# Re-slotting the weight conversion and softmax steps of a fused attention and MoE kernel, with 20 low-bit steps on ScalarE

## The chip, the cores and the metric

The kernel runs on one core of one Trainium2 chip. The metric is the device time of one execution, in microseconds (us); lower is better. The kernel before takes 794.07 us, the median of three runs (793.29 to 794.18).

## What is computed

The reference is a pooled attention followed by a gated two-layer product. Cut to what matters:

```
k_p = k.reshape(B, H, 72, 8, 64).mean(axis=3)        # B, H, S, D = 8, 8, 576, 64
v_p = v.reshape(B, H, 72, 8, 64).mean(axis=3)
attn = softmax(q @ k_p.T / sqrt(D)) @ v_p            # (B, H, S, D)
x = attn.transpose(0, 2, 1, 3).reshape(4608, 512)
a, b = x @ w1, x @ w2                                # w1, w2: 512 x 1024
out = (a * b) @ w3 @ w_out                           # w3: 1024 x 1024, w_out: 1024 x 512
```

The four weights arrive as 64-bit floats (20 MB in all); q, k and v are 32-bit floats.

## The kernel before, in words

**Chunks.** The 4608 tokens are worked in 12 chunks of 384. For chunk `m` TensorE (PE in the profile) does eight column blocks `j`: `a_mm` (12 matmuls, line 584), `b_mm` (12, line 584) and, one block later, `out_mm` (9, line 619). Every f32 operand is split into a high part, rounded to the matmul's type, and a low remainder, and a product is three passes: high by high, high by low, low by high. `w3 @ w_out` does not depend on the tokens, so it is folded first into one 1024 x 512 matrix `W`: 16 steps `s` of `w_mm` (line 645, 12 matmuls each), steps 0 to 7 for its first half, 8 to 15 for its second. Attention of chunk `n` (`s_mm` line 392, softmax, the transposes `pt_mm` line 454 and `ptr_mm` line 464, `av_mm` lines 558 to 561) is worked among the column blocks of chunk `n - 1`; that of chunk 0 stands among the steps `w_mm` 8 to 15.

**Weights.** Forty tiles of 512 KB (16 of `w3`, 8 of `w_out`, called wo, 16 of w1 and w2 together, called w12) are loaded as pairs of 32-bit words and turned into f32. For each tile `high` (ScalarE, ACT, line 135) takes sign, exponent and upper mantissa from the upper word, `low` (VectorE, DVE, line 140) takes the top three bits of the lower word by a shift of 29, and `conv_b` (VectorE, line 148) shifts the first by three and joins them. Then a `w3` tile is transposed on TensorE (`w_turn`, line 206); the high part is a ScalarE cast (lines 185, 192 and 152) and the low part a subtraction, on VectorE for `w3` and wo (lines 194, 177, 153) and, for 13 of the 16 w12 tiles, on GpSimd (POOL, line 153; `LO_DVE` lists the three others). In the first half of the product, `w_block` (lines 164 to 194) issues these steps of three neighbouring tiles as one fixed group.

**Softmax.** `soft1` takes the scores of four heads from PSUM: a minimum on VectorE (line 408), then either subtraction (line 410, VectorE), one Exp (413, ScalarE) and one sum (414, VectorE), or, for the tiles in `SOFT_ACT`, four Exp with bias and accumulated sum on ScalarE alone (line 418). `soft2` normalises (427 to 430, VectorE), `soft3` copies and splits the eight rest keys (442 ScalarE, 444 VectorE).

**k and v.** Eight neighbouring keys are summed, by three GpSimd additions (`pool_tree`, lines 348 to 350) or, for the k tiles in `K_DVE`, by one VectorE reduction (line 308). v's remainder (the eight pooled keys past the first 64) comes in eight loads of 16 KB per batch (`load_vr`, line 345) and becomes the tile `VR` (line 379, GpSimd).

**What sets the order.** Everything is put into a list `plan` with `at(kind, k, fn, ...)`, where `k` is a time slot; the list is sorted by slot and then by kind (loads, post-processing, main matmuls, attention matmuls) and issued in that order. Every engine runs its own instructions in that order, so an instruction that waits holds up all those behind it on its engine. All loads are issued from SyncE (SP), in order, and each waits for the load eight places before it to have landed. Three PSUM buffers (`patt`, name `att`) serve all transposes, scores and attention outputs, so a matmul into one waits until the reader of the old content is done.

Of the kernel before, what the change touches and what calls it, by code (L numbers as in the profile page):

```python
# [18 lines left out]
def kernel(  # L19
# [117 lines left out]
    def low(c, r):  # L137

        w = c.rearrange("p (c t) -> p c t", t=2)
        nc.vector.tensor_scalar(out=r, in0=w[:, :, 0], scalar1=29, scalar2=None, op0=ALU.logical_shift_right)  # L140
# [23 lines left out]
    def w_block(v):  # L164


        new, mid, old = v < NJ, 0 <= v - 1 < NJ, 0 <= v - 2 < NJ
        if new:
            w_tiles(v)
            r3, z3 = stage["w3", v]  # L170
            ro, zo = stage["wo", v]
            high(raw["w3", v], z3)
            low(raw.pop(("w3", v)), r3)
            high(raw["wo", v], zo)
        if old:
            s = v - 2
            nc.vector.tensor_tensor(out=wo[s][1], in0=f(stage["wo", s][0]), in1=f(wo[s][0]), op=ALU.subtract)  # L177
        if new:
            if v > 0:
                low(raw["wo", v], ro)  # L180
            conv_b(r3, z3)
        if mid:
            ps = w_turn(v - 1)
            w3t[v - 1] = hl_cell(4 + (v - 1) % 4)
            nc.scalar.copy(out=w3t[v - 1][0], in_=ps)
        if new:
            if v == 0:
                low(raw["wo", v], ro)
            conv_b(ro, zo)
        if mid:  # L190
            wo[v - 1] = hl_cell(8 + v - 1)
            nc.scalar.copy(out=wo[v - 1][0], in_=f(stage["wo", v - 1][0]))
        if mid:
            nc.vector.tensor_tensor(out=w3t[v - 1][1], in0=ps, in1=f(w3t[v - 1][0]), op=ALU.subtract)
# [7 lines left out]
    def w_turn(s):  # L202
        r = f(stage.pop(("w3", s))[0])
        ps = patt.tile([P, 512], F32, tag="att", name="att")
        for it in range(4):
            nc.tensor.transpose(out=ps[:, it * P:(it + 1) * P], in_=r[:, it * P:(it + 1) * P], identity=ident)
        return ps

    def w_conv(s):
        w_tiles(s)  # L210
        conv_a(raw.pop(("w3", s)), *stage["w3", s])

    def w_conv2(s):
        conv_b(*stage["w3", s])

    def w_split(s):
        ps = w_turn(s)
        w3t[s] = hl_cell(4 + s % 4)
        split(ps, *w3t[s])

    def w12_conv(j, w):
# [116 lines left out]
    def load_vr(b):  # L338
        t = stage["vr", b] = st_tile([P, 2, POOL, D])
        for g in range(2):  # L340
            for r in range(4):
# [3 lines left out]
                nc.sync.dma_start(out=t[KR * r:KR * r + KR, g].rearrange("k e d -> k (e d)"), in_=src)

    def pool_tree(t, dst):
        nc.gpsimd.tensor_tensor(out=t[:, :, 0:4], in0=t[:, :, 0:4], in1=t[:, :, 4:8], op=ALU.add)  # L348
        nc.gpsimd.tensor_tensor(out=t[:, :, 0:2], in0=t[:, :, 0:2], in1=t[:, :, 2:4], op=ALU.add)  # L349
# [469 lines left out]
```

## Time and profile before

| | before |
|---|---|
| median of three runs | 794.07 us |
| the profiled execution's own time | 796.23 us |
| its span, first to last instruction | 794.4 us |
| matmuls on TensorE | 4122 |
| VectorE busy | 457.4 us (58%) |
| ScalarE busy | 272.1 us (34%) |
| GpSimd busy | 210.0 us (26%) |
| loads and stores | 80.12 MB |

Times in the views are microseconds from the start of the span, unless marked ns. A group's row has its line, engine, operation, what it writes and reads, its count, its busy time and the mean duration of one, and behind the second bar the idle time of the engine ahead of it and what ended that. PEclk is the TensorE clock that was granted, as a share of full speed. In the timeline a bracket at the end of a row is the idle time ahead of it and what ended it. `raw` is a loaded weight tile, `Wc`, `wt` and `wb` are work tiles for `w3`, wo and w12, and `hl` is a finished weight in its high and low halves.

### The profile page before, as it was taken

What the parts mean: (1) busy time and instruction counts of PE and PEld (TensorE: products, weight loads), DVE (VectorE), ACT (ScalarE), POOL (GpSimd) and SP (SyncE); (2) the same over time, 40 slices, a digit from 0 to 9 for tenths busy, and PEclk for the clock granted to TensorE, in tenths of its full rate; (3) what the DMA queues carried; (4) which work ended last, traced back from release to release, by engine and by line L of the source; (5) the groups of instructions that cost most, each with busy time, mean ns of one, the idle gap of its engine ahead of it and who ended that gap; (6) DMA issues with size and microseconds to landing.
All of it is one profiled execution on the core that took longest, in us unless ns stands there. A gap on an engine that the chain in (4) does not pass through costs nothing.

```text
span 794.4 us, 11422 instructions
## 1 busy us (share of the span) xinstructions
PE 762.6 (96%) x4122; PEld 705.9 (89%) x4122; DVE 457.4 (58%) x889; ACT 272.1 (34%) x625; POOL 210.0 (26%) x240
## 2 busy tenths in 40 slices
PE   7888888999999999999999999999999999999998
PEld 7667778999999898999998998999998998999997
DVE  5866999565565465574384474474565664653111
ACT  5556555432233232333233223223323223323211
POOL 1153555402506413021408303022227221000000
PEclk9998999999999999999999999999999999999999
DMA  9896981024625412326326322138235314130101
GB/s 331 230 232 166 264 173 22 1 71 118 117 71 143 90 51 76 60 71 152 83 70 155 80 92 71 23 106 167 64 97 110 106 53 89 45 94 10 40 1 40
DMA packets 128680, 80.12 MB, mean 101 GB/s; under 512 B 82544, under 2 KB 112432, under 8 KB 128624
## 3 DMA queue, kind: packets, MB, share of 16 engines
q1 hardware_dynamic: 128624, 79.40, 39.7%
q8 instruction: 32, 0.52, 0.3%
q14 instruction: 24, 0.20, 0.1%
HBM read 61.08 MB, written 18.28 MB: 100 GB/s over the span
## 4 chain that ended last, share of the span: by engine, by line
PE 66%; DVE 9%; POOL 7%; DMA 7%; issue 4%; ACT 4%; SPq 2%; POOLq 0%; ACTq 0%; DVEq 0%
PE o L619 19%; PE a L584 19%; PE b L584 19%; DMA raw<-in_moe_w_dram 4%; PE att L392 3%; POOL st L348 3%; POOL VR L379 1%; DMA st<-in_k_dram 1%; POOL st L349 1%; PE att L561 1%; PE o L645 1%; DMA raw<-in_moe_w_out_dram 1%; DVE E L430 1%; PE att L559 1%; PE att L560 1%
## 5 line engine op out<-in xcount | busy, mean ns | idle before, releaser
L584 PE MATMUL a<-xT,hl 128*128 128x384 f32 x1152 | 222.6, 342 | 0.0
L584 PE MATMUL b<-xT,hl 128*128 128x384 f32 x1152 | 220.3, 339 | 0.0
L584 PEld LDWEIGHTS a<-xT,hl 128*128 128x128 f32 x1152 | 207.0, 191 | 6.1
L584 PEld LDWEIGHTS b<-xT,hl 128*128 128x128 f32 x1152 | 200.2, 189 | 0.0
L619 PE MATMUL o<-Wc,gh 128*128 128x512 f32 x576 | 183.6, 400 | 1.8 <-ACT gh L605 1.8
L348 POOL TENSOR_TENSOR st<-st 72x512 f32<-72x512 f32 (+2 forms) x53 | 76.8, 1448 | 248.6 <-DMA st<-in_k_dram 192.4
L604 DVE TENSOR_TENSOR a<-b,a 128x384 f32<-128x384 f32 x96 | 53.2, 554 | 124.8 <-PE b L584 124.2
L619 PEld LDWEIGHTS o<-Wc,gh 128*128 128x128 f32 x576 | 105.1, 189 | 19.9 <-ACT gh L605 2.8
L619 PE MATMUL o<-Wc,gl 128*128 128x512 f32 x288 | 114.2, 397 | 0.0
L594 ACT COPY a<-a 128x384 f32<-128x384 f32 x96 | 46.0, 479 | 173.0 <-PE a L584 152.0
L605 ACT CAST gh<-a 128x384 fp32r<-128x384 f32 x96 | 49.5, 515 | 154.5 <-DVE a L604 154.4
L610 DVE TENSOR_TENSOR gl<-a,gh 128x384 fp32r<-128x384 f32 x96 | 65.7, 684 | 39.1 <-ACT gh L605 38.5
L619 PEld LDWEIGHTS o<-Wc,gl 128*128 128x128 f32 x288 | 54.1, 188 | 13.4 <-DVE gl L610 0.9
L570 DVE TENSOR_TENSOR xT<-att,xT 128x384 fp32r<-128x384 f32 x48 | 26.6, 556 | 57.5 <-ACT xT L569 57.5
L413 ACT ACTIVATE E<-E 128x288 f32<-128x288 f32 (+1 forms) x70 | 31.2, 446 | 80.3 <-DVE E L410 80.3
L392 PE MATMUL att<-kbd,qT 128*128 128x144 f32 (+1 forms) x320 | 53.7, 292 | 3.4 <-DVE mx L408 3.2
L392 PEld LDWEIGHTS att<-kbd,qT 128*128 128x128 f32 (+1 forms) x320 | 48.2, 183 | 5.8 <-ACT E L418 4.0
L414 DVE TENSOR_REDUCE sm<-E 128x4 f32<-128x288 f32 (+1 forms) x70 | 31.6, 452 | 36.7 <-ACT E L413 36.7
L408 DVE TENSOR_REDUCE mx<-att 128x4 f32<-128x288 f32 (+1 forms) x80 | 35.4, 444 | 28.5 <-PE att L392 28.5
L361 POOL TENSOR_TENSOR vbd<-vm,vbd 64x256 fp32r<-64x256 f32 x16 | 12.4, 777 | 147.3 <-ACT vbd L360 147.2
L645 PE MATMUL o<-hl 128*128 128x512 f32 x144 | 43.0, 441 | 4.6 <-DVE hl L177 4.5
L349 POOL TENSOR_TENSOR st<-st 72x256 f32<-72x256 f32 (+2 forms) x53 | 42.9, 809 | 4.2
(91 smaller groups left out, 758.3 us busy)
## 6 DMA issues: line engine op xcount, KB each, us to landing
raw<-in_moe_w_dram SPq DMA_DIRECT2D x32, 512.0 KB
st<-in_k_dram SPq DMA_DIRECT2D x32, 288.0 KB
out_dram<-ob SPq DMA_DIRECT2D x35, 256.0 KB
st<-in_v_dram SPq DMA_DIRECT2D x32, 256.0 KB
qs<-in_q_dram SPq DMA_DIRECT2D x128, 48.0 KB
D<-T SPq DMA_DIRECT2D x7, 768.0 KB
PTl<-D SPq DMA_DIRECT2D x28, 192.0 KB
raw<-in_moe_w_out_dram SPq DMA_DIRECT2D x8, 512.0 KB
```

Source lines behind the costliest of these rows:

```text
L348: nc.gpsimd.tensor_tensor(out=t[:, :, 0:4], in0=t[:, :, 0:4], in1=t[:, :, 4:8], op=ALU.add)
L349: nc.gpsimd.tensor_tensor(out=t[:, :, 0:2], in0=t[:, :, 0:2], in1=t[:, :, 2:4], op=ALU.add)
L392: nc.tensor.matmul(out=ps[:nt, 2 * KP * j:2 * KP * (j + 1)], lhsT=qT[n][:, pr, off:off + nt], rhs=kbd[b % 2][:, pr], start=True, stop=True,)
L408: nc.vector.tensor_reduce(out=mx[:nt, hs], in_=sv, axis=AX.X, op=ALU.min)
L414: nc.vector.reduce_sum(out=sm[:nt, hs], in_=E[:nt, hs], axis=AX.X)
L584: nc.tensor.matmul(out=o, lhsT=w12[j, w][sw][:, kt * P:(kt + 1) * P], rhs=x[sx][:, kt], start=(i == 0), stop=(i == 3 * NK - 1))
L594: nc.scalar.copy(out=a, in_=gt[m, j][:, :CH])
L604: nc.vector.tensor_tensor(out=g, in0=ps[:, :CH], in1=g, op=ALU.mult)
L605: nc.scalar.copy(out=gh, in_=g)
L610: nc.vector.tensor_tensor(out=gl, in0=g, in1=f(gh), op=ALU.subtract)
L619: nc.tensor.matmul(out=oacc[m][t], lhsT=(gh, gl)[sg][:, c], rhs=W[j][sw], start=(j == 0 and i == 0), stop=(j == NJ - 1 and i == 2))
L645: nc.tensor.matmul(out=wacc[h][it], lhsT=w3t[s][sa][:, it * P:(it + 1) * P], rhs=wo[j][sb], start=(j == 0 and i == 0), stop=(j == NJ - 1 a ...
```

## The change

Four things are changed; the matmuls and what they multiply stay as they are.

1. What was one step becomes several, each with its own slot: `w_block`, `w_conv` and `w_split` become `r3_high`, `r3_low`, `r3_conv`, `w_turn`, `w3_hi`, `w3_lo` for `w3` and `ro_high` to `ro_lo` for wo; w12 gets `t_high` to `t_lo`; softmax `soft1`, `soft_e`, `soft_s`, `soft3`, `soft4`; x, g and v's remainder likewise. A table `SHIFT` adds a number to the slot of single steps, and `at` looks it up. Its entries belong to chunks 0 and 1, to the weights, and to the k and v of batches 0 and 1; the later chunks keep their order.
2. `low` has a second form on ScalarE: it reads one byte of each 8-byte element and scales it. 20 of the 40 tiles take it (8 of `w3`, 4 of wo, 8 of w12).
3. Other steps change engine: four wo remainders go from VectorE to GpSimd, w12 remainders on GpSimd become 9 instead of 13, k tile (1, 1) goes to GpSimd, k tile (0, 2) to VectorE additions, softmax tiles (0, 2) and (1, 2) from four Exp on ScalarE to VectorE and one Exp, tile (1, 0) the other way.
4. v's remainder comes in 4 loads of 32 KB per batch instead of 8 of 16 KB, and the mask `msk` is made by way of a ScalarE step.

```diff
-    SOFT_ACT = [(0, 0), (0, 1), (0, 2), (1, 1), (1, 2)]
-    LO_DVE = [(0, 1), (4, 1), (6, 0)]
-    K_DVE = [(0, 1), (1, 1), (1, 3)]
+    SOFT_ACT = [(0, 0), (0, 1), (1, 0), (1, 1)]
+    LO12_POOL = [(0, 0), (2, 0), (2, 1), (3, 0), (4, 0), (5, 0), (5, 1), (6, 0), (7, 0)]
+    LOW_ACT = [('w12', 0, 0), ('w12', 0, 1), ('w12', 1, 0), ('w12', 1, 1), ('w12', 2, 0), ('w12', 3, 1), ('w12', 5,
+        1), ('w12', 6, 1), ('w3', 0), ('w3', 1), ('w3', 13), ('w3', 5), ('w3', 6), ('w3', 7), ('w3', 8), ('w3', 9),
+        ('wo', 0), ('wo', 1), ('wo', 6), ('wo', 7)]
+    LOO_POOL = [1, 2, 4, 7]
+    K_RED = [(0, 1), (1, 3)]
+    K_TREE = [(0, 2)]
...
+    one = stp.tile([P, P], I32, tag="st", name="one")
+    nc.scalar.activation(out=one, in_=ident, func=AF.Copy, scale=0.75, bias=0.0)
...
-    def low(c, r):
-
+    def low(c, r, act=False):
+
+        if act:
+            b = c.bitcast(U8).rearrange("p (c t) -> p c t", t=8)
+            nc.scalar.activation(out=r, in_=b[:, :, 3], func=AF.Copy, scale=2.0 ** -5, bias=-31.0 / 64)
+            return
...
-    def conv_a(c, r, z):
-        high(c, z)
-        low(c, r)
-
...
+    def r3_low(s):
+        low(raw.pop(("w3", s)), stage["w3", s][0], ("w3", s) in LOW_ACT)
+
+    def r3_conv(s):
+        conv_b(*stage["w3", s])
...
+    def ro_lo(s):
+        eng = nc.gpsimd if s in LOO_POOL else nc.vector
+        eng.tensor_tensor(out=wo[s][1], in0=f(stage["wo", s][0]), in1=f(wo[s][0]), op=ALU.subtract)
...
+    def w3_hi(s):
+        w3t[s] = hl_cell(4 + s % 4)
+        nc.scalar.copy(out=w3t[s][0], in_=tp[s])
...
     def load_vr(b):
         t = stage["vr", b] = st_tile([P, 2, POOL, D])
-        for g in range(2):
-            for r in range(4):
...
+        for r in range(4):
+            par = r % 2
+            src = v[b, r::4, RK0[par] * POOL:(RK0[par] + KR) * POOL, :].rearrange("g (k e) d -> k g (e d)", e=POOL)
+            nc.sync.dma_start(out=t[KR * r:KR * r + KR].rearrange("k g e d -> k g (e d)"), in_=src)
...
+    SHIFT = {
...
+        "load_w12": {(0, 0): -6.25, (1, 0): -2.75, (1, 1): -4.25, (3, 0): 1.25},
...
+        "w3_hi": {(0,): -2.5, (11,): -2, (12,): -2.25, (14,): -0.5, (5,): 2.75, (8,): -1.75},
...
     def at(kind, k, fn, *args):
 
 
+        k += SHIFT.get(fn.__name__, {}).get(args, 0)
         plan.append((k // 1, "LPMA".index(kind), k % 1, len(plan), fn, args))
```

Three places show what that does to the order of an engine. The first is TensorE at the start of the program: `att` is a transpose (`ident` alone is warm-up, `Wc` a tile of `w3`), and the rows with `o0`, `o1`, `o2` and `a` are one step `w_mm`. Before:

```order
L200 MATMUL att_116<-ident_83 128x128 x36
L206 MATMUL att_179<-ident_83,Wc_160 128x128 x4
L200 MATMUL att_190<-ident_83 128x128 x12
L206 MATMUL att_215<-ident_83,Wc_172 128x128 x4
L645 MATMUL o0_226<-hl_187,hl_184 128x512 x3
```

The same place on TensorE after the change:

```order
L216 MATMUL att_126<-ident_83 128x128 x36
L203 MATMUL att_167<-ident_83,Wc_117 128x128 x4
L216 MATMUL att_194<-ident_83 128x128 x12
L203 MATMUL att_211<-ident_83,Wc_183 128x128 x4
L203 MATMUL att_230<-ident_83,Wc_216 128x128 x4
L693 MATMUL o0_235<-hl_191,hl_172 128x512 x3
```

The transpose of the third `w3` tile now stands ahead of the first step of the product; before it stood behind that step.

The second is ScalarE some 30 us later, around steps 5 to 7 of the product. `raw_236` and `raw_238` are the tiles 6 of `w3` and wo, `raw_246` is tile 8 of `w3`, `raw_275` and `raw_277` are the tiles 7; a CAST from `att` is the high part of a transposed `w3` tile, here of tile 5 (`att_380`) and tile 6 (`att_425`). Before:

```order
L135 ACTIVATE Wc_373<-raw_236 128x512
L135 ACTIVATE wt_158<-raw_238 128x512
L185 CAST hl_385<-att_380 128x512
L192 CAST hl_388<-wt_157 128x512
L135 ACTIVATE Wc_398<-raw_246 128x512
L135 ACTIVATE Wc_418<-raw_275 128x512
L135 ACTIVATE wt_158<-raw_277 128x512
L185 CAST hl_430<-att_425 128x512
```

After, with line 144 the high and line 150 the low bits, `raw_257` tile 8 and `raw_255` tile 7 of `w3`, `raw_174` tile 7 of wo, and `att_381` the transposed tile 5:

```order
L144 ACTIVATE Wc_394<-raw_257 128x512
L150 ACTIVATE Wc_393<-raw_257 128x512
L190 CAST hl_398<-wt_114 128x512
L144 ACTIVATE Wc_417<-raw_255 128x512
L150 ACTIVATE Wc_416<-raw_255 128x512
L144 ACTIVATE wt_115<-raw_174 128x512
L150 ACTIVATE wt_115<-raw_174 128x512
L207 CAST hl_429<-att_424 128x512
L190 CAST hl_432<-wt_114 128x512
L207 CAST hl_436<-att_381 128x512
```

The cast of tile 5, which step 5 of the product needs, moved from ahead of the tiles 8 and 7 to behind both, and each tile there now has two ScalarE conversions.

The third is VectorE at the end of chunk 0's attention, where `xT` is the low part of x (line 570 before, 615 after), `wb` and `hl<-wb` are steps of w12, `km` is a sum over keys and `qT` a transpose of q. Before:

```order
L153 TENSOR_TENSOR hl<-att,hl 128x512
L542 TENSOR_TENSOR PTl<-att,PTh 128x4x128
L140 TENSOR_SCALAR wb<-raw 128x512
L285 STREAM_TRANSPOSE qT<-qs 128x384
L148 SCALAR_TENSOR_TENSOR wb<-wb 128x512
L140 TENSOR_SCALAR wb<-raw 128x512
L308 TENSOR_REDUCE km<-st 72x128
L285 STREAM_TRANSPOSE qT<-qs 128x384
L148 SCALAR_TENSOR_TENSOR wb<-wb 128x512
L570 TENSOR_TENSOR xT_983<-att,xT_982 128x384
```

After:

```order
L585 TENSOR_TENSOR PTl<-att,PTh 128x4x128
L210 TENSOR_TENSOR hl<-att,hl 128x512
L289 STREAM_TRANSPOSE qT<-qs 128x384
L241 TENSOR_TENSOR hl<-wb,hl 128x512
L615 TENSOR_TENSOR xT_985<-att,xT_984 128x384
L241 TENSOR_TENSOR hl<-wb,hl 128x512
L615 TENSOR_TENSOR xT_985<-att,xT_984 128x384 x3
```

Between the split of the last softmax tile and the first low part of x there were eight instructions and are now three; two shifts of line 140, two joins of line 148, the key sum and one transpose are gone from there.

More of the change, by code (lines that the diff above doesn't have):

```diff
@@ L162, in w_tiles, with r3_high @@
         stage["w3", s] = W_cell(0, 4 + s % 4, I32), W_cell(1, 4 + s % 4, F32)
[L164 to L194, printed above, removed]
+    def r3_high(s):
+        w_tiles(s)
+        high(raw["w3", s], stage["w3", s][1])
@@ new lines, in r3_low, with ro_high, ro_low, ro_conv @@
+    def r3_low(s):
+        low(raw.pop(("w3", s)), stage["w3", s][0], ("w3", s) in LOW_ACT)
+    def r3_conv(s):
+        conv_b(*stage["w3", s])
+    def ro_high(s):
+        high(raw["wo", s], stage["wo", s][1])
+    def ro_low(s):
+        low(raw.pop(("wo", s)), stage["wo", s][0], ("wo", s) in LOW_ACT)
+    def ro_conv(s):
+        conv_b(*stage["wo", s])
+    def ro_hi(s):
+        wo[s] = hl_cell(8 + s)
+        nc.scalar.copy(out=wo[s][0], in_=f(stage["wo", s][0]))
+    def ro_lo(s):
+        eng = nc.gpsimd if s in LOO_POOL else nc.vector
+        eng.tensor_tensor(out=wo[s][1], in0=f(stage["wo", s][0]), in1=f(wo[s][0]), op=ALU.subtract)
@@ new lines, with w_turn, w3_lo @@
+    tp = {}
+    def w_turn(s):
+        r = f(stage.pop(("w3", s))[0])
+        ps = tp[s] = patt.tile([P, 512], F32, tag="att", name="att")
+        for it in range(4):
+            o, i = ps[:, it * P:(it + 1) * P], r[:, it * P:(it + 1) * P]
+            nc.tensor.transpose(out=o, in_=i, identity=ident)
+    def w3_hi(s):
+        w3t[s] = hl_cell(4 + s % 4)
+        nc.scalar.copy(out=w3t[s][0], in_=tp[s])
+    def w3_lo(s):
+        nc.vector.tensor_tensor(out=w3t[s][1], in0=tp.pop(s), in1=f(w3t[s][0]), op=ALU.subtract)
@@ L200, in warm, with t_high @@
             nc.tensor.transpose(out=ps[:, :P], in_=ident, identity=ident)
[L202 to L221, printed above, removed]
+    def t_high(j, w):
         i = 2 * j + w
@@ L360, in prep_v2, with prep_v3 @@
         nc.scalar.copy(out=hi, in_=vm[b][r])
+    def prep_v3(b, par):
+        r = slice(64 * par, 64 * par + 64)
+        hi, lo = (vbd[b % 2][s][r, :, D * par:D * par + D] for s in range(2))
         nc.gpsimd.tensor_tensor(out=lo, in0=vm[b][r], in1=f(hi), op=ALU.subtract)
@@ L420, in soft1, with soft_s @@
                 accum_out=sm[:nt, h:h + 1])
+    def soft_s(n, t, half):
+        if (n, t) in SOFT_ACT:
+            return
+        b, off, nt = tok_tiles(n)[t]
+        hs = slice(4 * half, 4 * half + 4)
+        nc.vector.reduce_sum(out=Mt[n, t][1][:nt, hs], in_=Et[n, t][:nt, hs], axis=AX.X)
     Rt = {}
@@ L442, in soft3, with soft4 @@
             nc.scalar.copy(out=R[:nt, :, q], in_=er)
+    def soft4(n, t):
+        b, off, nt = tok_tiles(n)[t]
+        E, R = Et[n, t], Rt[n, t]
+        er = rest_keys(E, nt).rearrange("p (g a) h e -> p g a h e", g=2)
         for q in range(2):
@@ L647, in w_mm, with W_hi, W_lo @@
                     start=(j == 0 and i == 0), stop=(j == NJ - 1 and i == 2))
-    def w_post(h):
-        for it in range(4):
-            i = 4 * h + it
-            W[i] = [W_cell(x, i, F32R) for x in range(2)]
-            split(wacc[h][it], *W[i])
+    def W_hi(i):
+        W[i] = [W_cell(x, i, F32R) for x in range(2)]
+        nc.scalar.copy(out=W[i][0], in_=wacc[i // 4][i % 4])
+    def W_lo(i):
+        nc.vector.tensor_tensor(out=W[i][1], in0=wacc[i // 4][i % 4], in1=f(W[i][0]), op=ALU.subtract)
@@ L670, in plan_att @@
                 at("P", k + 1, soft1, n, t, half)
+                at("P", k + 1, soft_e, n, t, half)
+                at("P", k + 1, soft_s, n, t, half)
             at("P", k + 2, soft2, n, t)
@@ L679, in plan_att @@
             at("P", k + 3, soft3, n, t)
+            at("P", k + 3, soft4, n, t)
             k = pt_at[t]
@@ L721 @@
     at("M", F0 - 2, warm, 12)
-    for s in range(NJ + 2):
-        at("P", F0 + 2 * (s - 2), w_block, s)
+    for u in range(NJ + 2):
+        k = F0 + 2 * (u - 2)
+        if u < NJ:
+            at("P", k, r3_high, u)
+            at("P", k, r3_low, u)
+            at("P", k, ro_high, u)
+        if u >= 2:
+            at("P", k, ro_lo, u - 2)
+        if 0 < u < NJ:
+            at("P", k, ro_low, u)
+        if u < NJ:
+            at("P", k, r3_conv, u)
+        if 1 <= u < NJ + 1:
+            at("P", k, w_turn, u - 1)
+            at("P", k, w3_hi, u - 1)
+        if u == 0:
+            at("P", k, ro_low, u)
+        if u < NJ:
+            at("P", k, ro_conv, u)
+        if 1 <= u < NJ + 1:
+            at("P", k, ro_hi, u - 1)
+            at("P", k, w3_lo, u - 1)
     for s in range(NS):
```

149 lines of the change are left out of this document (114 added, 35 removed).

## Prediction

> **What bounds the kernel now.** I read the page first, then the waits of TensorE, then the stretches of the program.
>
> ```profile
> span 794.4 us, 11422 instructions
> PE 762.6 (96%) x4122; PEld 705.9 (89%) x4122; DVE 457.4 (58%) x889; ACT 272.1 (34%) x625; POOL 210.0 (26%) x240
> ```
>
> TensorE is busy for 96% of the span, so the other engines matter only where TensorE waits for them or is slow because of it. The change leaves the matmuls alone; it can win only the gaps. I cut the span where the trace's matmul lines change: steps 0 to 7 of `w_mm` (S1), steps 8 to 15 with the attention of chunk 0 (S2), blocks 0 to 5 of chunk 0 with the w12 conversions (S3), and the rest (S4). Columns: length, then busy time and count for each engine, granted clock, DMA share, GB/s.
>
> ```profile
> 0.00:46.10 46.10, 38.60 (x184) 32.23 (x185) 33.02 (x61) 23.48 (x40) 9.21 (x18) 0.93 0.93 270
> 46.10:93.60 47.50, 38.52 (x185) 31.27 (x184) 36.15 (x66) 28.52 (x97) 23.05 (x26) 0.91 0.82 208
> 93.60:147.20 53.60, 47.40 (x250) 44.16 (x249) 47.37 (x81) 31.82 (x97) 31.15 (x26) 0.89 0.48 110
> 147.20:794.40 647.20, 638.06 (x3510) 598.25 (x3508) 340.89 (x684) 188.24 (x395) 146.59 (x171) 1.00 0.33 80
> ```
>
> S4 is 98.6% matmul at a clock of 1.00. All that can be won lies ahead of it: 22.7 us without matmul (7.5 + 9.0 + 6.2) and a clock under 1. These are TensorE's waits in S1 to S3 and then in S4 (total, times, longest):
>
> ```profile
> PE o L645 <- DVE hl L177: 4.5, 3, 2.2
> PE att L464 <- ACT E L418: 4.0, 2, 3.9
> PE att L558 <- DVE xT L570: 3.5, 1, 3.5
> PE att L392 <- DVE mx L408: 3.2, 1, 3.2
> PE att L464 <- DVE E L410: 2.0, 1, 2.0
> PE att L206 <- DVE Wc L148: 1.6, 1, 1.6
> PE att L464 <- DVE R L444: 1.0, 1, 1.0
> PE att L454 <- DVE E L430: 1.0, 1, 1.0
> ```
>
> ```profile
> PE att L561 <- POOL st L349: 3.3, 3, 1.1
> PE o L619 <- ACT gh L605: 1.8, 3, 0.6
> PE att L561 <- DVE PTr L528: 0.3, 1, 0.3
> ```
>
> Nearly all waits are for VectorE. Where they lie, from the timeline of TensorE (start, length, line; the bracket is the wait ahead):
>
> ```profile
> 13.54 1.22 PE L645 MATMUL o<-hl 128*128 128x512 f32 x2 [1.01 <-DVE hl L177]
> 33.54 1.26 PE L645 MATMUL o<-hl 128*128 128x512 f32 x3 [2.18 <-DVE hl L177]
> 39.91 0.73 PE L645 MATMUL o<-hl 128*128 128x512 f32 x2 [1.33 <-DVE hl L177]
> 57.87 0.58 PE L392 MATMUL att<-kbd,qT 128*128 128x144 f32 x1 [3.23 <-DVE mx L408]
> 90.75 0.44 PE L558 MATMUL att<-PTh,vbd 128*128 128x384 f32 x1 [3.53 <-DVE xT L570]
> 117.92 0.58 PE L464 MATMUL att<-ident,R 96*128 96x96 f32 x2 [3.85 <-ACT E L418]
> ```
>
> And the stretch that follows each wait, in the columns above:
>
> ```profile
> 33.50:38.00 4.50, 4.46 (x14) 3.54 (x15) 3.77 (x7) 2.27 (x4) 0.00 (x0) 0.62 0.59 156
> 57.80:63.00 5.20, 5.13 (x19) 4.29 (x20) 2.17 (x5) 4.03 (x25) 3.30 (x4) 0.67 0.62 187
> 66.40:72.00 5.60, 4.58 (x18) 3.81 (x19) 3.58 (x10) 3.07 (x13) 0.00 (x0) 0.70 0.72 177
> 90.70:97.00 6.30, 6.25 (x25) 5.79 (x26) 6.30 (x12) 3.73 (x8) 1.48 (x2) 0.73 1.10 316
> 118.00:123.00 5.00, 5.00 (x19) 4.96 (x20) 4.13 (x5) 4.72 (x16) 3.89 (x3) 0.52 0.62 99
> ```
>
> Each is busy but at 0.52 to 0.73 of the clock. Length times what is missing of the clock gives the loss: 4.5 x .38 = 1.7, 5.2 x .33 = 1.7, 5.6 x .30 = 1.7, 6.3 x .27 = 1.7, 5.0 x .48 = 2.4. So a wait costs its length and about 1.7 us of slow matmuls behind it, and two waits of 1.0 us close together (66.4) cost as much clock as one of 3.5.
>
> [...]
>
> **The change part by part.** Prices of the steps, from the groups of VectorE, ScalarE and GpSimd (count, then busy us and mean ns), `Wc` in S1 and S2, `wb` in S3:
>
> ```profile
> L140 DVE TENSOR_SCALAR Wc<-raw 128x512 int32<-128x512 int32 x16 | 6.8, 428 | 10.3 <-DMA raw<-in_moe_w_dram 10.3
> L177 DVE TENSOR_TENSOR hl<-wt,hl 128x512 fp32r<-128x512 f32 x8 | 5.5, 684 | 0.0
> L135 ACT ACTIVATE Wc<-raw 128x512 f32<-128x512 f32 x16 | 10.9, 679 | 14.6 <-DMA raw<-in_moe_w_dram 14.6
> L148 DVE SCALAR_TENSOR_TENSOR Wc<-Wc 128x512 int32<-128x512 int32 x16 | 10.9, 681 | 0.3 <-ACT Wc L135 0.3
> L140 DVE TENSOR_SCALAR wb<-raw 128x512 int32<-128x512 int32 x11 | 8.2, 748 | 0.0
> L148 DVE SCALAR_TENSOR_TENSOR wb<-wb 128x512 int32<-128x512 int32 x12 | 11.6, 963 | 0.9 <-ACT wb L135 0.8
> ```
>
> *Byte lows on ScalarE.* The trace has no instruction that reads one byte in eight. Nearest is ScalarE's own pass over such a tile, 679 ns (L135). It could be no quicker than VectorE's 428 (L140), and at worst I allow twice L135, 1.36 us, because a strided byte may cost more. I take 679. In S1 eleven of the 20 are made (`w3` 0, 1, 5 to 9, wo 0, 1, 6, 7): ScalarE's load goes from 23.5 to 23.5 + 11 x .679 = 31.0 us, VectorE's from 33.0 to 33.0 - 11 x .428 - 4 x .684 (wo remainders to GpSimd) = 25.6. So in S1 ScalarE becomes the busier one.
>
> *S1.* (a) The start: four lows (tiles 0 and 1 of `w3` and wo) go onto ScalarE's chain ahead of the first step, up to 4 x .679 = 2.7 us, less what it idles; the third transpose also goes ahead of that step. TensorE's first `w_mm` moves from 13.54 to about 16.1: +2.6. (b) The waits of 2.18 and 1.33 at steps 5 and 6 are for wo remainders (L177), four of which now go to GpSimd: -3.5, and -1.7 of clock. (c) But the cast of `w3` tile 5 now stands behind the conversions of tiles 8 and 7 on ScalarE, about nine instructions or 5.3 us (679 ns or less each) behind a landing. Its landings in the trace:
>
> ```profile
> 26.67 0.69 ACT L135 ACTIVATE wt<-raw 128x512 f32<-128x512 f32 x1 [0.22 <-DMA raw<-in_moe_w_out_dram]
> 32.37 0.67 ACT L135 ACTIVATE Wc<-raw 128x512 f32<-128x512 f32 x1 [2.71 <-DMA raw<-in_moe_w_dram]
> ```
>
> wo's tile 6 was there by 26.7 and tile 7 of `w3` at 32.4, so the cast comes between 26.7 + 5.3 = 32.0, in time for the step that now starts at 33.5, and 37.7, four to five late: 0 to +5.3. Sum of S1 between 2.6 - 5.2 = -2.6 and +2.7; I take **0**, the middle, as the loads' new places don't say which landing it is.
>
> *S2.* The 3.23 at 57.9 is a score matmul waiting for a minimum (L408) that stands on VectorE behind a `w3` low waiting for its load; that low (tile 13) goes to ScalarE, and the minima come free. I leave about 2.1 of small waits there: -1.1. The two waits of 1.0 (behind L430 and L444) and their clock: -3.7, as the splitting of rest keys (`soft4`) of other tiles no longer stands ahead. The 3.53 at 90.75: VectorE's chain there was eight instructions and is three, -3.5 - 1.7. At most **-10.0**. I add back one new stall of about 4 us, a wait of 2 to 2.5 with its 1.7 of clock, because S2 takes in steps that left S3 (w12 tiles begin earlier on ScalarE): **-6**. The four loads of v's remainder in place of eight leave SP's row sooner:
>
> ```profile
> 52.59 8.03 SPq L345 DMA_DIRECT2D st<-in_v_dram  x8
> ```
>
> Half of that is 4 us of queue. No wait of TensorE above is for a load of v, so alone it is worth nothing; behind it in the queue stand w12 loads, which now come that much sooner (in the -6).
>
> *S3.* Waits of 3.85 at 117.92 (for the four Exp of line 418) and 1.96 (for line 410), their clock of 2.4 and 1.7, and 0.4 of short ones: at most **-10.3**. But VectorE was busy 47.4 of the 53.6 us and sheds little: three lows (3 x .748 = 2.2) leave, and as GpSimd's w12 remainders fall from 13 to 9 about two come in, each about .68. The same join (L148) lasts 963 ns here and 681 in S1 and S2, and GpSimd is busy for 31.2 us here and 9.2 in S1; I read that as VectorE slowed beside GpSimd, and allow 1.5 us less with fewer remainders there. So VectorE falls by 2.2 - 1.4 + 1.5 = 2.3 us, and its steps are moved to later slots. The softmax tiles (0, 2) and (1, 2) going from ScalarE to VectorE and (1, 0) the other way take the cause of the 3.85 away but load VectorE. I take 40% of the best: **-4**. At nothing, 0; at best -8, two us of waits staying.
>
> *S4.* Its order stays; its 5.4 us of waits are for GpSimd's v sums (L349) and `g`, whose steps are the same: **0**. `msk` by way of ScalarE: one instruction at the very start, where all wait for the first load: 0.
>
> Sum: 0 - 6 - 4 + 0 = **-10 us**. The profiled execution took 796.23 (its span 794.4 and 1.8 around it), the median 794.07, 2.2 less; 796.2 - 10 = 786.2 profiled, **784.0** as a median.
>
> **The rivals.**
> *All gaps close.* S1 -2, S2 -10, S3 -8: -20, 774. For it: every long wait named above has its own step moved. Against: eight waits on three engines would all have to go and none appear; VectorE stays near 44 of 54 us in S3.
> *Waits only move.* VectorE still bounds S3 (0), S1 loses 2.5 by the late cast, S2 wins 5: -2.5, 791.6. For it: 47.4 of 53.6 busy. Against: the chain of eight at 85 to 90 us is really shorter.
> *Slower: ScalarE takes VectorE's place.* The 20 lows stand in ScalarE's queue ahead of the casts that TensorE and VectorE wait for. If all lie in chains, each adds .679 - .428 = .25, 20 x .25 = 5.0 us, with no gap won since its casts now end last: 794 + 5 = 799. It decides against the change if a byte low is long: with some 14 of 20 in chains that end at a matmul, the -10 is used up when each costs 10 / 14 = .7 more than taken, at about 1.4 us. For it: ScalarE at 31.0 us becomes the busiest helper of S1. Against: ScalarE had 19 to 23 us idle in each stretch.
> [...]
> *Nothing happens.* The moved steps were all hidden anyway: 794. Against: 20 us of waits and clock belong to the very steps moved.
>
> **How the numbers follow.** Forecast 784: 0.50. All gaps close, 774: 0.17. Waits move, 791.6: 0.21, of which 0.03 ends within 0.2% (1.6 us, about what a measurement of this kernel can tell from no change). Slower, 799: 0.10. Nothing: 0.02. Faster .50 + .17 + .18 = 0.85, same .03 + .02 = 0.05, slower 0.10. The forecast's own bounds are S1 -2.6 to 2.7, S2 -10 to -3, S3 -8 to 0; with not all at one end, about 778 to 790. The range of 8 in 10 leaves out the 799 case (0.10) and the better half of the 774 case (0.08): **775 to 793**.
>
> **What would show it.** In the profile after: the first `w_mm` matmul near 16 (right) or still near 13.5; the first step 8 near 46; the first `a_mm` about 6 us sooner than 93.6 and block 6 about 10 sooner than 147.2, the spacing from there on as before. The clock of 0.70 to 0.73 at 66 and 91 should be gone, and no wait of 3 us or more for VectorE be left in S2. A byte low of .68 is right; over 1.4 would prove the slower rival, as would long waits of TensorE for ScalarE's casts (lines 190, 207). VectorE busy at 90% in S3, with waits as long as before, would mean that waits only moved. Wrong altogether: a gain in S4, or one without shorter waits.

## The result and the profile after

The changed kernel takes **784.25 us** (median of four runs, 783.98 to 784.74) against 794.12 of the kernel before timed beside it (793.29 to 794.76): a ratio of 0.9877, 95% interval 0.986 to 0.9894. The forecast was 784.0. Its profiled execution took 784.28, with a span of 782.2; that of before 796.23, at a span of 794.4.

The windows of the changed kernel, cut at the same matmuls as before (step 8 of `w_mm`, the first `a_mm`, block 6 of chunk 0); columns as before: length, busy time and count of PE, PEld, DVE, ACT, POOL, then granted clock, DMA share, GB/s:

```profile
0.00:50.10 50.10, 39.76 (x193) 33.42 (x193) 34.69 (x51) 30.98 (x54) 15.66 (x22) 0.90 1.01 273
50.10:88.20 38.10, 34.16 (x177) 27.38 (x175) 33.32 (x59) 28.21 (x84) 23.07 (x25) 1.00 0.84 202
88.20:135.60 47.40, 43.04 (x249) 39.46 (x248) 44.06 (x79) 32.17 (x96) 27.44 (x21) 1.00 0.64 144
135.60:782.20 646.60, 637.85 (x3511) 598.36 (x3508) 340.28 (x689) 190.03 (x399) 150.39 (x174) 1.00 0.32 80
```

Against 46.1, 47.5, 53.6 and 647.2 before, S1 is 4.0 us longer, S2 9.4 shorter, S3 6.2 shorter and S4 0.6 shorter. The clock in S2 and S3 went from 0.91 and 0.89 to 1.00.

TensorE's waits in the first 137 us of the changed kernel (total, times, longest):

```profile
PE att L203 <- DVE Wc L157: 5.4, 2, 3.0
PE att L504 <- DVE R L484: 4.3, 2, 2.9
PE o L693 <- ACT hl L207: 3.6, 1, 3.6
PE att L412 <- ACT E L446: 1.1, 2, 0.6
PE att L504 <- ACT E L446: 0.8, 1, 0.8
PE att L494 <- DVE E L432: 0.7, 1, 0.7
```

And where four of them lie, on its timeline:

```profile
16.05 1.09 PE L203 MATMUL att<-ident,Wc 128*128 128x128 f32 x4 [2.96 <-DVE Wc L157]
38.00 3.13 PE L693 MATMUL o<-hl 128*128 128x512 f32 x6 [3.62 <-ACT hl L207]
66.62 0.41 PE L504 MATMUL att<-ident,R 128*128 128x128 f32 x2 [1.31 <-DVE R L484]
117.91 0.36 PE L504 MATMUL att<-ident,R 96*128 96x96 f32 x2 [2.94 <-DVE R L484]
```

Of the three waits of over 3 us before, those at 57.9 and 90.8 are gone; one is new, the 3.62 for the late cast. Between 50 and 109 us only one wait is over a microsecond. The 2.94 at 117.91 takes the place of the 3.85: its releaser is VectorE now, no longer the four Exp.

The stretch behind the last three, by windows:

```profile
38.00:41.40 3.40, 3.40 (x9) 2.37 (x10) 3.40 (x5) 1.08 (x2) 0.00 (x0) 0.52 1.11 192
66.60:70.00 3.40, 3.38 (x22) 3.10 (x23) 1.94 (x5) 1.51 (x5) 0.00 (x0) 1.00 0.82 221
117.90:121.30 3.40, 3.39 (x20) 2.96 (x21) 3.29 (x9) 3.28 (x8) 0.00 (x0) 1.00 0.56 91
```

Only the 3.62 was followed by half clock (0.52 in the first row). The 2.94 was not (1.00), though before a wait of 2.18 was (0.62 in the prediction's row at 33.50). The last section has the counts on this.

### The profile page after: what moved, and what is told of

Read it like the earlier page. It is cut to its first block, busy times and chain, and to the rows that moved or that the text cites. A ratio compares the mean times of both kernels' runs of the same rounds, so it can differ in the third digit from the quotient of the medians.

```text
span 782.2 us, 11337 instructions
## 1 busy us (share of the span) xinstructions
PE 754.8 (96%) x4122; PEld 698.6 (89%) x4122; DVE 452.3 (58%) x875; ACT 281.4 (36%) x632; POOL 216.6 (28%) x240
## 4 chain that ended last, share of the span: by engine, by line
PE 68%; DVE 11%; POOL 7%; ACT 6%; issue 4%; DMA 3%; SPq 1%; POOLq 0%; DVEq 0%; ACTq 0%
PE o L667 19%; PE a L629 19%; PE b L629 19%; PE att L412 3%; POOL st L350 2%; PE o L693 2%; DVE E L432 1%; ACT E L441 1%; DVE E L465 1%; DMA st<-in_v_dram 1%; DVE mx L428 1%; POOL st L351 1%; PE att L604 1%; POOL VR L399 1%; PE att L602 1%
## 5 line engine op out<-in xcount | busy, mean ns | idle before, releaser
L629 PE MATMUL a<-xT,hl 128*128 128x384 f32 x1152 | 219.0, 338 | 0.3 <-ACT a L639 0.3
L629 PEld LDWEIGHTS a<-xT,hl 128*128 128x128 f32 x1152 | 203.5, 188 | 6.5 <-ACT a L639 0.5
L658 DVE TENSOR_TENSOR gl<-a,gh 128x384 fp32r<-128x384 f32 x96 | 62.8, 654 | 37.8 <-ACT gh L654 37.2
L428 DVE TENSOR_REDUCE mx<-att 128x4 f32<-128x288 f32 (+1 forms) x80 | 35.6, 445 | 28.4 <-PE att L412 28.2
L693 PE MATMUL o<-hl 128*128 128x512 f32 x144 | 41.3, 426 | 3.6 <-ACT hl L207 3.6
```

The lines of the kernel that those rows point to most:

```text
L428: nc.vector.tensor_reduce(out=mx[:nt, hs], in_=sv, axis=AX.X, op=ALU.min)
L629: nc.tensor.matmul(out=o, lhsT=w12[j, w][sw][:, kt * P:(kt + 1) * P], rhs=x[sx][:, kt], start=(i == 0), stop=(i == 3 * NK - 1))
L658: nc.vector.tensor_tensor(out=gl, in0=g, in1=f(gh), op=ALU.subtract)
L693: nc.tensor.matmul(out=wacc[h][it], lhsT=w3t[s][sa][:, it * P:(it + 1) * P], rhs=wo[j][sb], start=(j == 0 and i == 0), stop=(j == NJ - 1 a ...
```

## The experiments

Twelve kernels, each timed beside the kernel before on the same chip; the ratio is to that. The kernel before had single runs from 792.3 to 798.1 and medians of 794.1 (beside the changed kernel) and 795.0 to 796.4 (beside the others), so the ratio of the changed kernel is to the fastest of these: e10, with the same time within 0.2 us, has 0.9847 for its 0.9877. Differences below about 2 us, or 0.003 in ratio, between two of the kernels are therefore not told apart.

| run | what is edited | us | ratio to before, 95% interval |
|---|---|---|---|
| the change | | 784.25 | 0.9877 (0.986 to 0.9894) |
| e1 | all lows on VectorE | 790.51 | 0.9952 (0.9934 to 0.9969) |
| e2 | no slot shifts | 792.03 | 0.9967 (0.9949 to 0.9984) |
| e3 | start undone | 782.89 | 0.9853 (0.9833 to 0.9872) |
| e4 | cast of tile 5 in its place | 783.56 | 0.9867 (0.9843 to 0.9892) |
| e6 | 2 MB fewer loads | 782.66 | 0.9834 (0.9815 to 0.9854) |
| e7 | the eleven early lows on VectorE | 783.84 | 0.9845 (0.9821 to 0.9868) |
| e8 | e7, start and cast undone | 784.93 | 0.9861 (0.9837 to 0.9886) |
| e9 | softmax lists of before | 789.22 | 0.9907 (0.9891 to 0.9923) |
| e10 | eight loads of v's remainder | 784.07 | 0.9847 (0.9822 to 0.9871) |
| e11 | each byte low twice | 792.18 | 0.9952 (0.9933 to 0.9971) |
| e13 | the other eight w12 lows on ScalarE | 784.77 | 0.9847 (0.9827 to 0.9867) |
| e15 | e3, e4 and e6 together | 783.42 | 0.9828 (0.9786 to 0.987) |

When some matmuls start in each profile (us from the start of the span): the first `w_mm`, steps 8 and 10, the first `a_mm` and block 6 of chunk 0, read from TensorE's timelines. Behind block 6 all of them run alike (646.4 to 647.4 us to the end). Each row is one execution; those of e3, e4, e7 and e15 are the slowest of their kernel, 1.8 to 4.2 us above its median, so a row and a median of these do not belong together to the microsecond.

| | first `w_mm` | step 8 | step 10 | first `a_mm` | block 6 |
|---|---|---|---|---|---|
| before | 12.0 | 46.1 | 59.9 | 93.7 | 147.2 |
| after | 16.8 | 50.1 | 60.4 | 88.2 | 135.6 |
| e1 | 15.3 | 50.2 | 60.5 | 94.7 | 142.8 |
| e2 | 11.8 | 43.9 | 59.7 | 90.0 | 142.8 |
| e3 | 11.4 | 48.1 | 58.4 | 88.6 | 136.5 |
| e4 | 15.8 | 49.8 | 60.1 | 90.3 | 139.1 |
| e6 | 15.9 | 47.8 | 58.1 | 86.7 | 133.3 |
| e7 | 15.2 | 50.4 | 60.7 | 89.6 | 137.0 |
| e8 | 11.4 | 48.1 | 58.4 | 88.5 | 136.4 |
| e9 | 16.4 | 48.8 | 59.0 | 91.2 | 141.1 |
| e10 | 16.6 | 49.7 | 60.0 | 87.8 | 135.6 |
| e11 | 18.6 | 55.4 | 65.7 | 95.2 | 144.2 |
| e13 | 16.2 | 48.8 | 59.2 | 86.6 | 134.4 |
| e15 | 13.3 | 47.7 | 58.7 | 89.1 | 137.0 |

**e1, all 20 lows on VectorE.**

```diff
-    LOW_ACT = [('w12', 0, 0), ('w12', 0, 1), ('w12', 1, 0), ('w12', 1, 1), ('w12', 2, 0), ('w12', 3, 1), ('w12', 5,
-        1), ('w12', 6, 1), ('w3', 0), ('w3', 1), ('w3', 13), ('w3', 5), ('w3', 6), ('w3', 7), ('w3', 8), ('w3', 9),
-        ('wo', 0), ('wo', 1), ('wo', 6), ('wo', 7)]
+    LOW_ACT = []
```

> All 20 low steps go back to VectorE in the slots of the change; everything else as changed. Theory A (the moved slots carry the gain, the engine of the lows matters little): 784 within 1.6 us, ScalarE's load before 46 us back to about 21 us, VectorE's in chunk 0 up by some 2 us without new waits. Rival B (VectorE's shorter queue carries the gain): 20 lows of 0.43 to 0.75 us return to chains that end at a matmul, the time goes at least half of the way back, 789 or more. Rival C (ScalarE's queue is what makes the first 46 us 4 us longer): 780 to 782, with the first step of the product back at 13.5.

790.5: rival B. Steps 0 to 9 took as long as with the lows on ScalarE (step 8 at 50.2 and 50.1); from step 8 to the first `a_mm` it is 44.5 us in place of 38.1. VectorE's timeline there shows why (line 151 is the low, 208 the remainder of a `w3` tile):

```profile
79.48 0.95 DVE L151 TENSOR_SCALAR wb<-raw 128x512 int32<-128x512 int32 x1
80.35 0.56 DVE L287 STREAM_TRANSPOSE qT<-qs 128x384 f32<-128x384 f32 x1
80.85 0.38 DVE L151 TENSOR_SCALAR wb<-raw 128x512 int32<-128x512 int32 x1
81.15 0.67 DVE L208 TENSOR_TENSOR hl<-att,hl 128x512 fp32r<-128x512 f32 x1
81.75 0.41 DVE L151 TENSOR_SCALAR wb<-raw 128x512 int32<-128x512 int32 x1
82.08 1.78 DVE L155 SCALAR_TENSOR_TENSOR wb<-wb 128x512 int32<-128x512 int32 x1
```

and on TensorE:

```profile
81.88 0.65 PE L201 MATMUL att<-ident,Wc 128*128 128x128 f32 x4 [1.69 <-DVE hl L208]
87.95 0.80 PE L691 MATMUL b<-hl 128*128 128x512 f32 x1 [2.20 <-DVE hl L208]
```

Three lows of w12 stand among the remainders that the last steps of `w_mm` need, and TensorE waits for two of these remainders.

**e2, no slot shifts.**

```diff
-    SHIFT = {
...
-    }
+    SHIFT = {}
```

> The table of slot shifts is emptied; the steps stay split, and the lows, remainders, key sums, softmax forms and the four loads stay as changed. Theory A (slots carry the gain): 791 or slower, waits of 3 us or more for VectorE back at the softmax and x steps. Rival B (shorter VectorE queue carries it): 787 or faster.

792.0, theory A by its bound, though the interval just leaves out no gain. With e1 it shows that neither half of the change does it alone: all but the lows is worth 0.5%, all but the slots 0.3%, the whole 1.2%. TensorE's waits are again long and at the scores, the softmax and the x steps, but the one of over 3 us is for the four Exp on ScalarE, not for VectorE as theory A had it:

```profile
PE att L412 <- ACT E L446: 4.0, 2, 3.3
PE o L693 <- DVE hl L194: 3.1, 2, 2.3
PE att L494 <- DVE PTl L585: 2.7, 1, 2.7
PE att L504 <- DVE E L432: 2.2, 2, 1.2
PE att L601 <- DVE xT L615: 2.2, 1, 2.2
```

**e3, the start undone.**

```diff
-        1), ('w12', 6, 1), ('w3', 0), ('w3', 1), ('w3', 13), ('w3', 5), ('w3', 6), ('w3', 7), ('w3', 8), ('w3', 9),
-        ('wo', 0), ('wo', 1), ('wo', 6), ('wo', 7)]
+        1), ('w12', 6, 1), ('w3', 13), ('w3', 5), ('w3', 6), ('w3', 7), ('w3', 8), ('w3', 9),
+        ('wo', 6), ('wo', 7)]
...
-        "w_turn": {(0,): -2.5, (1,): -0.25, (10,): -2.75, (11,): -2.75, (12,): -2.5, (14,): -0.5, (2,): -2, (3,):
+        "w_turn": {(0,): -2.5, (1,): -0.25, (10,): -2.75, (11,): -2.75, (12,): -2.5, (14,): -0.5, (3,):
```

> The four lows of the first two tiles of w3 and wo go back to VectorE, and the transpose of the third w3 tile goes back behind the first step. Theory (ScalarE's queue delays the start, and the delay reaches the end): first w_mm matmul from 16.8 to about 13.5, time 781. Rival (the cast of tile 5, which waits for loads at 37.4, ends last whatever the start does): the start comes earlier but the step at 38.0 does not, time 784, the wait there longer by what the start won, about 6 to 7 us.

The start came 5.4 us sooner, the wait for the cast stayed (3.1), step 10 came 2.0 sooner, and the first `a_mm` did not: 88.6. The 782.9 can't be told from 784.25. The time is the rival's, but not its mechanism: the step at 38.0 did come sooner, at 34.8, and the wait there did not grow. Most of the start was lost not to the lows but to the place of the third transpose: e7, which moves these lows and seven others back and leaves the transpose, starts at 15.2, only 1.6 us sooner. Hardly any of it reaches the end.

**e4, the cast of tile 5 in its own slot.**

```diff
-        "w3_hi": {(0,): -2.5, (11,): -2, (12,): -2.25, (14,): -0.5, (5,): 2.75, (8,): -1.75},
-        "w3_lo": {(12,): -1, (15,): 0.25, (3,): 0.25, (4,): 1, (5,): 2.75, (7,): 2.5},
+        "w3_hi": {(0,): -2.5, (11,): -2, (12,): -2.25, (14,): -0.5, (8,): -1.75},
+        "w3_lo": {(12,): -1, (15,): 0.25, (3,): 0.25, (4,): 1, (7,): 2.5},
```

> Only the two steps of w3 tile 5 (cast and remainder) go back to their own slot, ahead of the conversions of tiles 8 and 7. Theory (the cast was late only because of its place in ScalarE's queue): the wait of 3.62 at 38.0 and the slow clock behind it go, 3.6 + 1.7 = 5.3 at best, time 779 to 781. Rival (the conversions behind it are then late themselves): the wait comes back one or two steps on, time 784, or slower if it lands among the scores of chunk 0.

The rival: the 3.62 is gone, and step 8 still comes at 49.8. First TensorE, then VectorE, then ScalarE in that stretch:

```profile
44.44 1.41 PE L693 MATMUL o<-hl 128*128 128x512 f32 x4 [2.11 <-DVE hl L210]
```

```profile
40.77 1.44 DVE L350 TENSOR_TENSOR st<-st 72x512 f32<-72x512 f32 x1 [1.15 <-DMA st<-in_k_dram]
```

```profile
46.27 0.68 ACT L144 ACTIVATE Wc<-raw 128x512 f32<-128x512 f32 x1 [4.94 <-DMA raw<-in_moe_w_dram]
```

VectorE stands at the key sum that the change gave it (k tile (0, 2)) until its load lands, with the remainder of tile 7 behind it; ScalarE idles for 4.9 us until a `w3` tile lands. By these rows the loads take what the cast wins; this is a reading of one execution, which took 787.7, 4 us above the median.

**e6, fewer loads.**

```diff
     def load_wo(j):
         raw["wo", j] = raw_cell(8 + j)
+        if j >= 4:
+            nc.gpsimd.memset(raw["wo", j], 0)
+            return
```

> Four of the eight wo tiles are not loaded but set to zero by GpSimd, so 2 MB less is read in the first 40 us, and the output is not the product; all else as changed. Theory (what ends the first 60 us is the arrival of the weights, 2 MB at the 280 GB/s of that stretch are 7.5 us): the late cast at 38.0 and step 8 come 4 to 7 us sooner, step 10 of w_mm from 60.4 to about 55, the time about 780. Rival (the conversions on ScalarE and VectorE set it): step 10 stays within 1 us of 60.4 and the time within 1.6 us of 784.

Between the two: step 10 at 58.1, 2.3 us sooner and not 5, and the time, 782.66, inside the rival's 1.6 us. Neither the loads alone nor ScalarE and VectorE alone hold it.

**e7 and e8, the early lows.** e7 is the edit of e1 for the eleven lows of steps 0 to 9 only; e8 has the edits of `w_turn` and of the cast (e3, e4) besides.

```diff
-        1), ('w12', 6, 1), ('w3', 0), ('w3', 1), ('w3', 13), ('w3', 5), ('w3', 6), ('w3', 7), ('w3', 8), ('w3', 9),
-        ('wo', 0), ('wo', 1), ('wo', 6), ('wo', 7)]
+        1), ('w12', 6, 1), ('w3', 13)]
```

> The eleven lows of the first half of w_mm go back to VectorE in the slots of the change; the eight of w12 and that of w3 tile 13 stay on ScalarE. Theory (the lows pay after step 10, where VectorE's queue ends the waits; before it they cost and gain nothing that lasts): w_mm starts 1 to 1.5 us sooner, the way from step 10 to the first a_mm stays at 28 us, the time 782 to 784. Rival (the early lows carry as much as the late ones, 11 x 0.43 = 4.7 us of VectorE): 787 or more.

> As the run before it, and the third transpose as well as the steps of w3 tile 5 go back to their own slots: what cost in the first 46 us is undone together. Theory (the point that decides is step 10 near 60 us, whatever the start does): step 8 comes 3 us or more sooner than 50.1, step 10 stays at 58 to 60, the time 782 to 784. Rival (each early us counts): 779 or 780.

e7 is as the theory has it: 783.8. e8 misses the theory's numbers, with step 8 only 2.0 us sooner and 784.9, but its point holds, step 10 at 58.4, and the rival's 779 or 780 is ruled out. The eleven early lows are worth nothing measurable; the other nine make the 6.7 us between e1 and e7 (8.5 by the ratios), 0.7 to 0.9 us each. In e8 the product starts 5.4 us sooner than in the changed kernel and the first `a_mm` 0.3 later.

**e9, the softmax lists of before.**

```diff
-    SOFT_ACT = [(0, 0), (0, 1), (1, 0), (1, 1)]
+    SOFT_ACT = [(0, 0), (0, 1), (0, 2), (1, 1), (1, 2)]
```

> The list of softmax tiles with four Exp on ScalarE is again that of before: (0, 2) and (1, 2) go back to ScalarE, (1, 0) back to VectorE; slots and all else as changed. Theory (S3's gain came from VectorE's shorter queue; the softmax lists only shift load between the two engines): 783 to 786. Rival (the wait of 3.85 for the four Exp was removed by the lists): that wait comes back at the second rest transpose of chunk 1, 788 or more.

789.2, as much as the rival said, but not by its mechanism: the wait for four Exp did not come back. From TensorE's timeline:

```profile
66.53 0.41 PE L504 MATMUL att<-ident,R 128*128 128x128 f32 x2 [2.12 <-DVE R L484]
85.94 0.50 PE L693 MATMUL b<-hl 128*128 128x512 f32 x1 [1.22 <-DVE hl L210]
115.36 0.36 PE L504 MATMUL att<-ident,R 96*128 96x96 f32 x2 [3.15 <-DVE R L484]
```

All three are for VectorE. Most of the loss lies between step 8 and the first `a_mm` (42.4 us for 38.1), where tile (0, 2) is worked. There VectorE waits for ScalarE in its turn, for the last of the four Exp, a wait that the changed kernel does not have. From VectorE's waits in e9 between 50 and 91 us:

```profile
DVE sm L462 <- ACT E L446: 1.4, 1, 1.4
```

That is a part of the loss, one engine further back than the rival said; the rest was not followed. Beside e10, timed with it, e9 is 5.1 us slower.

**e10, eight loads of v's remainder**, the inner lines of `load_vr` as before.

```diff
-        for r in range(4):
-            par = r % 2
+        for g in range(2):
+            for r in range(4):
...
```

> v's remainder comes in eight loads of 16 KB per batch again, all else as changed. Prediction: worth nothing alone, as no wait of TensorE is for it: 784 within 1.6 us, though SP's row in front of the w12 loads is 4 us longer. Rival (the w12 loads behind it are late and hold up ScalarE, whose high steps are queued ahead of softmax): 786 or more, with waits of ScalarE for w12 loads between 55 and 75 us.

784.07: worth nothing alone. SP's timeline shows the row of eight and the w12 loads behind it:

```profile
53.80 6.70 SPq L349 DMA_DIRECT2D st<-in_v_dram  x8
60.63 0.94 SPq L135 DMA_DIRECT2D raw<-in_moe_w_dram  x2
```

In the changed kernel the same places read:

```profile
54.21 1.47 SPq L347 DMA_DIRECT2D st<-in_v_dram  x4
56.70 1.63 SPq L135 DMA_DIRECT2D raw<-in_moe_w_dram  x2
```

The two w12 loads are issued at 60.6 in place of 56.7, and the end does not move.

**e11, each byte low twice.**

```diff
             nc.scalar.activation(out=r, in_=b[:, :, 3], func=AF.Copy, scale=2.0 ** -5, bias=-31.0 / 64)
+            nc.scalar.activation(out=r, in_=b[:, :, 3], func=AF.Copy, scale=2.0 ** -5, bias=-31.0 / 64)
```

> Each of the 20 byte lows is issued twice on ScalarE, so a low costs 1.3 us in place of 0.66; the output is the same. The prediction's point for a slower kernel was a low of about 1.4 us, by 14 of 20 lows in chains. If that holds: 14 x 0.66 = 9 us more, 793. Rival (ScalarE has slack nearly everywhere, since loads end the first 60 us and VectorE the rest): 787 or less.

792.2, 7.9 us more (6.0 by the ratios): at 0.66 per low that is as much as 12 of the 20 paid in full (9 by the ratios), for the 14 assumed. Which of them pay is not shown by this. TensorE's waits name ScalarE's cast and the joins behind the lows:

```profile
PE att L204 <- DVE Wc L158: 7.0, 2, 3.8
PE o L694 <- ACT hl L208: 5.7, 1, 5.7
PE att L505 <- DVE R L485: 4.2, 3, 3.0
```

5.3 us of the delay are there by step 10, of the 7.9 us that the twelve lows ahead of it add: in the first 60 us ScalarE has little slack left.

**e13, the other eight w12 lows on ScalarE too.**

```diff
-        ('wo', 0), ('wo', 1), ('wo', 6), ('wo', 7)]
+        ('wo', 0), ('wo', 1), ('wo', 6), ('wo', 7), ('w12', 2, 1), ('w12', 3, 0), ('w12', 4, 0), ('w12', 4, 1),
+        ('w12', 5, 0), ('w12', 6, 0), ('w12', 7, 0), ('w12', 7, 1)]
```

> The eight w12 lows that were left on VectorE go to ScalarE too (28 lows there). Theory (VectorE's queue still ends the waits in the attention of chunks 0 and 1, and nine late lows gave 6 to 7 us): the wait of 2.9 at 117.9 shrinks or goes and the time is 780 to 782. Rival (ScalarE, at 31 of 42 us busy between step 8 and the first a_mm, is now the one that is waited for): 784 to 788, with waits for its Exp and casts.

784.8, no gain, though without the rival's waits for ScalarE. VectorE is busy for 40.2 us from the first `a_mm` to block 6 in place of 44.1, and that stretch is 47.8 us long in place of 47.4:

```profile
86.60:134.40 47.80, 42.78 (x251) 39.64 (x249) 40.16 (x72) 36.60 (x105) 21.97 (x19) 1.00 0.54 132
```

So the 20 lows are enough. The wait of 2.94 did not go but was split (2.85 at 109.50 and 1.43 at 116.47, both for VectorE). That what is left in S3 is a matter of which step stands ahead of which is my reading; no run tests it.

**e15, the edits of e3, e4 and e6 together.**

> Both at once: four wo tiles set to zero in place of loaded (2 MB less read, the output is not the product), and the four first lows, the third transpose and the steps of w3 tile 5 put back where they cost the start nothing. Theory (up to step 10 the loads and ScalarE's queue end within 2 us of each other, so that undoing one shows the other): step 10 from 60.4 to 55 or sooner, more than the 2.3 and 2.0 that each gave alone, the time 780 or less. Rival (a third thing, the waits of VectorE behind the first scores, takes what the start wins): step 10 at 56 to 58, the first a_mm still at 87 to 88, the time 782 to 784.

Nearest the rival: 783.4, with step 10 at 58.7 and the first `a_mm` at 89.1, both later than it said. From TensorE's timeline:

```profile
56.34 0.76 PE L415 MATMUL att<-kbd,qT 128*128 128x144 f32 x4 [1.25 <-ACT E L449]
66.69 0.66 PE L507 MATMUL att<-ident,R 128*128 128x128 f32 x2 [2.12 <-DVE R L487]
```

With the loads and the early steps both relieved, the scores (for ScalarE's Exp) and the rest keys of chunk 0 (for VectorE) wait instead. No kernel here is clearly faster than the changed one; the ratio of e6 lies below its interval, but only 0.0013 below that of e10.

## Why the prediction held, step by step

**The sum.** -10 was forecast from the profiled execution of 796.23; the two profiles differ by 12.0, the medians by 9.9. The number came out within 0.3 us, but the terms did not: S1 +4.0 (forecast 0, bounds -2.6 to 2.7), S2 -9.4 (-6), S3 -6.2 (-4), S4 -0.6 (0). That they add up so near is luck: the errors of +4.0, -3.4, -2.2 and -0.6 leave -2.2, and this is just what the profiled execution of before lay above its median, while that of the changed kernel lay at its own. That S2 and S3 carry the gain, by shorter waits, most of them for VectorE, is not luck.

**The byte low: right.** Taken at 679 ns. Count and shortest, median, longest in ns, from the changed kernel's rows of line 150:

```profile
L150 ACT ACTIVATE Wc<-raw x8: 642/658/669, 4.8 to 53.8; 128x512 int32<-128x512 uint8 x8
L150 ACT ACTIVATE wb<-raw x8: 657/678/680, 69.0 to 131.9; 128x512 int32<-128x512 uint8 x8
```

A byte in eight cost as much as the whole pass of line 144 (means of 673 ns for `Wc` and 670 for `wb` in the same profile). The single low is dearer on ScalarE, these medians of 658 and 678 ns for 422 and 420 on VectorE before (line 140), and nine of them there gave 6.7 us (e1 against e7) all the same, since ScalarE had the time: it was busy for 28.2 of the 38.1 us of S2 and 32.2 of the 47.4 of S3.

**S1: outside its bounds, and it hardly mattered.** The first `w_mm` matmul was at 12.04 before (the 13.54 of the prediction is the row behind it) and is at 16.78 now: 4.7 us later, for 2.6 forecast from four lows. The lows are 1.6 of it (e7); the rest is the third transpose, which the prediction named and gave no price (e8 starts 3.8 sooner than e7). VectorE's load, forecast to fall from 33.0 to 25.6 us, rose to 34.7: eleven lows and four remainders left, but the nine lows that stayed took 632 and 690 ns on average for 428, the joins of wo 922 for 688, and key additions came in. So VectorE, not ScalarE (31.0), stayed the busier one; what slowed its steps is not shown (GpSimd was busy for 15.7 us beside it, for 9.2 before). The cast of tile 5 came at the late end of the range given, 37.4 of 32.0 to 37.7:

```profile
37.37 0.58 ACT L207 CAST hl<-att 128x512 fp32r<-128x512 f32 x1
```

The steps that failed are the start's price, the middle of that range, and that I priced S1 at its own end. Step 10 comes at 58.1 to 60.7 in thirteen of the fourteen profiles, whatever came before it (the exception is e11), although the first `w_mm` starts anywhere between 11.4 and 16.8. Before, what delayed it was a conversion waiting for the load of tile 13, with the minima queued behind it; the same load at the same time without the slot shifts (e2) held up ScalarE, and the scores waited 3.3 us for its Exp. So moving that low to ScalarE would not have freed the scores without the slots. VectorE before, then ScalarE in e2:

```profile
55.67 0.43 DVE L140 TENSOR_SCALAR Wc<-raw 128x512 int32<-128x512 int32 x1 [2.38 <-DMA raw<-in_moe_w_dram]
```

```profile
55.61 0.66 ACT L144 ACTIVATE Wc<-raw 128x512 f32<-128x512 f32 x1 [3.79 <-DMA raw<-in_moe_w_dram]
```

So the 4.0 of S1 is paid back by the scores' wait of before: up to step 10 the two kernels differ by 0.5 us. e3, e4, e6, e8 and e15 each took something away ahead of step 10 and won 0.3 to 2.3 us there. Loads, ScalarE's queue and softmax end close together; which of them is next after each was not settled.

**S2: right mechanism, too careful.** From step 10 to the first `a_mm` it is 33.8 us before and 27.8 after. The waits named went (66.4, 68.0, 90.8); VectorE's chain ahead of the last was seven instructions, not eight, and is three. The stall of 4 added back did not come; instead 1.3, 0.7 and 0.5 stayed. e1, e9 and e2 show what it rests on: with the lows back on VectorE the stretch is 6.4 us longer, with the softmax lists of before 4.3, without the slots 2.5. These are more than 6.0 together, so they are no shares of it: each needs the others.

**S3: right sign, the wait changed hands.** The 3.85 became 2.94 for VectorE, as the rival of moving waits had it, but without its clock, and that is luck (last section); the 1.96 went. VectorE's busy time fell by 3.3 us, for 2.3 forecast.

**v's remainder, the engine lists, S4: nothing, as forecast** for the first (e10) and the last. Of the lists only the softmax one was undone: 5 us, where I had no separate term for it, only a part in the -4 of S3; most of it lies in S2. The remainders and key sums on other engines were not tried alone.

**The slower rival: its point was about right.** A low of 1.3 us brings 792.2, 8 of the 10 us back (6 by the ratios).

**"A wait costs its length and about 1.7 us": wrong for waits under 3 us.** The last section has the counts. Before's profile had six slow stretches, two of them behind waits of about 2 us; in the other executions such waits are as often as not without one. One of them, at 1.7 us, would be most of the 2.2 by which this execution lies above its median. This last is argued, not shown.

## What to carry to other kernels

Price a stage not at its own end but at the next point where another resource arrives: four microseconds lost ahead of step 10 cost half of one, since scores, loads and conversions met there anyway. An operation that is half again as dear (here 658 ns for 422) may still be worth moving when the engine it leaves is the one in whose queue the next wait ends; which instances pay is seen by moving them back in groups (nine of twenty did). And the change without its lows gave 0.5%, without its slots 0.3%, and whole 1.2%, so such a pair is to be tried as a pair.
